# RWKV attention and a SoLU block on one core: w by ScalarE's queue, work moved between engines at the start, and another order at the end

## The chip, the core and the metric

The kernel runs on one core of a Trainium2 chip. A core has five instruction streams: TensorE (PE, the matrix unit; its weight loads are listed apart as PEld), VectorE (DVE), ScalarE (ACT), GpSimd (POOL) and SyncE (SP, which here only issues DMAs). Each stream runs in program order, and streams wait for one another by semaphores. The metric is the time of one execution on the device, in microseconds.

## The reference

The input is r, k, v of shape (4, 8, 768, 48), w and u of shape (8, 48), and the weights of a feed-forward block. Attention first:

```python
state = zeros((B, H, D, D))
for t in range(S):
    cur = einsum('bhd,bhe->bhde', u[None] * k[:, :, t], v[:, :, t])
    y[:, :, t] = einsum('bhd,bhde->bhe', r[:, :, t], state + cur)
    state = w[None, :, :, None] * state + einsum('bhd,bhe->bhde', k[:, :, t], v[:, :, t])
```

Its output, as 3072 rows of 384, then goes through

```python
h = x @ w_in                       # (3072, 1024)
e = exp(h - max(h)); sm = e / (sum(e) + 1e-9)
solu = h * sm
ln = (solu - mean(solu)) / sqrt(var(solu) + 1e-6) * g_ln
out = ln @ w_out                   # (3072, 384)
```

The feed-forward weights arrive as 64-bit floating-point words; the rest is 32-bit.

## The kernel before

The sequence is cut into 24 units (`units`): 6 chunks of 128 time steps for each of 4 batch rows, in the order chunk by chunk. A unit has all 8 heads. Each engine's order is the order of the calls in the code, written out by hand (`tc.manual_schedule()`): there is no planner.

**Preparing.** Powers of w and their inverses are made as tables once (lines 634 to 655): w is loaded into `wq` (line 493), turned by TensorE (`wd_ps`, line 636), and VectorE builds `pw` and `tab` (whose halves are `back` and `fore`) by repeated doubling. TensorE turns `back` into `kdec`, copied by ScalarE (line 665). u is loaded as one row (line 496), spread over 128 rows by a matmul with `ones_row` (line 638) and copied by ScalarE to `u_bc` (line 639). `ident`, the identity matrix, is made by GpSimd, as are the masks. The second halves of six value tiles `vts` are zeroed by ScalarE (line 641). `spin` issues filler matmuls on `ident` whose output nobody reads.

**Attention of a unit.** GpSimd decays k (`decay_k`, line 721) and makes the own products r·u·k (`weigh`, lines 734 and 735); VectorE sums them over each head (`sum_own`, 739). `diagonal` puts the sums on the diagonal of the score matrix: on ScalarE (749) for the first four units, later on GpSimd (754). `turn_r` and `turn_k` turn r and k by TensorE, with a VectorE product (779, 790) or a ScalarE copy (788) on the way out. Scores come from TensorE (801, 819), and VectorE's predicated copies (827, 832) put them above the diagonal. `whole_y` (858) or `merged_y` (881) makes the output, `whole_outer` (922) or `outer` (913) the contribution to the state. In both forms `take_y` copies the transposed result to `xT`.

**Feed-forward of a unit.** `ffn_in` (969) multiplies by w_in; from unit 17 on pairs of units do it with 11 instead of 12 blocks (lines 1003 on). Exponential and sum are ScalarE's (977), solu VectorE's (`unit_a`, 1049 and 1053), the sum of squares ScalarE's (`unit_b`, 1061 or 1065). `deviation` then makes the inverse deviation on GpSimd: a scale and offset (1073), a power of -0.5 (1075), and for units from 4 on a scale and a shift (1079, 1081) which `normalise` (1093) applies on ScalarE. `halve_ln` (1118) splits each 32-bit word in two halves, SyncE issues a turning DMA (1107), and `join_ln` (1112) on VectorE puts the words together. The output product is done for two units at a time with 7 instead of 8 block products (`both_a` to `both_d`, all matmuls on line 1202), which need sums of rows (`row_sums_12`, `row_sums_34`, lines 1192 to 1198).

**Weights.** 14 pieces (6 of w_in, 8 of w_out) are loaded by SyncE (524) and converted to 32 bits in steps: `convert_a` on ScalarE (537), `convert_b` on VectorE (550, 552), `convert_c` on GpSimd (560) and, for w_out alone, `convert_d`, a scaling by -g on ScalarE (568) or VectorE (571). The loop over i = 2 to 6 (line 1390) converts two w_out pieces in each round. Later every piece is loaded again and checked: `check_next` runs ScalarE's sum (582) on one piece and issues the load of the next, `check_least` takes VectorE's minimum (590), and `compare_sums` with `check_sums` ends in one flag, made by a matmul (706).

**Around the change.** At the start the order is: the loads, `ident`, three fillers, tables, u, zeroing, `turn_r(0)`, `turn_k(0)`, `kdec`, `wide` (1313), `weigh(0)`, `decay_k(0)`, and the units 0, 1, 2 interleaved with the conversion of w_in. At the end (lines 1763 to 1821) the last two pairs, 20/21 and 22/23, wait for the norm of unit 23.

Of the kernel before, what the change touches and what calls it, by code (L numbers as in the profile page):

```python
# [399 lines left out]
def direct_path(  # L400
# [89 lines left out]
    w_out_sb = const.tile([128, KF, dm], F32, name="w_out_sb")  # L490
    decays = const.tile([128, HP], F32, name="decays")

    nc.gpsimd.dma_start(out=wq[:, :, 0:D], in_=w.rearrange("(a q) d -> a q d", q=2))
    nc.vector.memset(wq[:, :, D:], 1.0)
    u_row = u_bc[0:1].rearrange("p h d -> p (h d)")
    nc.scalar.dma_start(out=u_row, in_=u.rearrange("h d -> (h d)").unsqueeze(0))
# [66 lines left out]
    def convert_d(j, scalar=False):  # L563
        dst, _, f = pieces[j]
        ma, low = step.pop(j)
        if f is not None:
            if scalar:
                nc.scalar.activation(out=dst, in_=ma.bitcast(F32), func=ACT.Copy,
                                     scale=minus_g[:, f : f + 1])
            else:  # L570
                nc.vector.tensor_scalar_mul(out=dst, in0=ma.bitcast(F32),
                                            scalar1=minus_g[:, f : f + 1])
# [64 lines left out]
    u_ps = psM.tile([128, dm], F32, tag="m", name="u_ps")  # L637
    nc.tensor.matmul(u_ps, ones_row, u_row, start=True, stop=True)
    nc.scalar.copy(out=u_bc.rearrange("p h d -> p (h d)"), in_=u_ps)
    for vt in vts:  # L640
        nc.scalar.activation(out=vt[:, 1].rearrange("p h x -> p (h x)"),
                             in_=ident[:, 0:1].to_broadcast([128, H * P]), func=ACT.Copy, scale=0.0)
    nc.vector.tensor_scalar(out=pw[:, 0, 0], in0=wd_ps, scalar1=LOW, scalar2=HIGH,
# [64 lines left out]

    ones = const.tile([128, 1], F32, name="ones")
    nc.gpsimd.memset(ones, 1.0)  # L710

    live = {}

# [4 lines left out]
    def decay_k(i):  # L718
        X = live.setdefault(i, {})
        X["kp"] = apool.tile([128, H, P], F32, name="kp", bufs=5)  # L720
        nc.gpsimd.tensor_mul(X["kp"].rearrange("p h d -> p (h d)"),  # L721
                             kpads[i % NLD].rearrange("p h d -> p (h d)"),
                             kdec.rearrange("p a d -> p (a d)"))
# [5 lines left out]
                             rpads[i % NLD].rearrange("p h d -> p (h d)"),  # L729
                             rdec.rearrange("p a d -> p (a d)"))  # L730

    def weigh(i, engine):
        rku = live[i]["rku"] = apool.tile([128, H, D], F32, name="rku")
        engine.tensor_mul(rku, kpads[i % NLD][:, :, 0:D], u_bc)  # L734
        engine.tensor_mul(rku, rku, rpads[i % NLD][:, :, 0:D])  # L735

    def sum_own(i):
        own = live[i]["own"] = small.tile([128, H, 1], F32, name="own")
# [329 lines left out]
        unit_a(i)  # L1068
        unit_b(i)

    def deviation(i, j):
        ss, var, rstd = (stats[:, n, i:j] for n in (2, 3, 4))
        nc.gpsimd.tensor_scalar(out=var, in0=ss, scalar1=1.0 / dff, scalar2=1e-6 * dff ** 2,  # L1073
                                op0=ALU.mult, op1=ALU.add)
        nc.gpsimd.tensor_tensor(out=rstd, in0=var, in1=neg_half.to_broadcast([128, j - i]), op=ALU.pow)
        i = max(i, SEVEN)
        if i < j:
            tot, shift, scale, rstd = (stats[:, n, i:j] for n in (1, 2, 3, 4))
            nc.gpsimd.tensor_scalar(out=scale, in0=rstd, scalar1=-float(dff), scalar2=1.0,
                                    op0=ALU.mult, op1=ALU.mult)  # L1080
            nc.gpsimd.tensor_tensor(out=shift, in0=tot, in1=rstd, op=ALU.mult)  # L1081

    def normalise_late(i):
        if SEVEN <= i < N:
# [4 lines left out]
    def normalise(i):  # L1089

        if SEVEN <= i < N:
            solu = live[i]["solu"]
            nc.scalar.activation(out=solu, in_=solu, func=ACT.Identity,  # L1093
                                 scale=stats[:, 3, i : i + 1], bias=stats[:, 2, i : i + 1])
# [26 lines left out]
    def join_ln(i):  # L1121
        X = live[i]
        if i not in ROOM:
            X["lnT"] = fpool.tile([128, KF, 128], F32, name="lnT")
        else:
            X["lnT"] = bigs[ROOM[i]].rearrange("p (f t) -> p f t", f=KF)
        join(X["lnT"], X["turned"])
# [85 lines left out]
    def both_a(i, which=(0, 1, 2)):  # L1213
        X = live[i]
        if 0 in which:
            X["o"], X["o2"] = rows_out(i), rows_out(i + 1)
            X["a"], X["e"] = (psM.tile([128, NH], F32, tag="m", name="o_ps") for _ in range(2))
            block(X["a"], X["lnT"][:, 0:KH], upper[:, :, left], True)
            X.get("copy", nc.scalar.copy)(out=X["o"][:, left], in_=X["a"])
        if 1 in which:  # L1220
            block(X["e"], X["lnT"][:, KH:KF], lower[:, :, left], True)
        if 2 in which:
            block(X["a"], X["s"][2], sums_w[2])
# [8 lines left out]
    def both_b(i, between=None, later=False):  # L1232
        X = live[i]
        block(X["e"], X["s"][1], sums_w[1], True)
        X.get("copy", nc.scalar.copy)(out=X["o2"][:, right], in_=X["e"])
        if not later:
            both_b2(i, between)
# [8 lines left out]
    def both_c_sum(i, also=False):  # L1246
        X = live[i]
        o2 = X["o2"]
        nc.vector.tensor_tensor(out=o2[:, right], in0=X["a"], in1=o2[:, right], op=ALU.add)
        X["summed"] = True  # L1250
        if also:
            o = X["o"]
            nc.vector.tensor_tensor(out=o[:, right], in0=X["e"], in1=o[:, right], op=ALU.add)
            X["summed"] = 2

    def both_c(i):
        X, Y = live.pop(i), live.pop(i + 1)
        ending[i] = X
        o, o2, a, e = (X[n] for n in ("o", "o2", "a", "e"))
        rows, rows2 = (out[ds(b * S + c * T, T)] for b, c in (units[i], units[i + 1]))  # L1260
        if not X.get("summed"):
            nc.vector.tensor_tensor(out=o2[:, right], in0=a, in1=o2[:, right], op=ALU.add)
        block(a, Y["lnT"][:, KH:KF], sums_w[4])
        if i + 2 == N:
            nc.sync.dma_start(out=rows2[:, right], in_=o2[:, right])
        if X.get("summed") != 2:
            nc.vector.tensor_tensor(out=o[:, right], in0=e, in1=o[:, right], op=ALU.add)
        nc.sync.dma_start(out=rows, in_=o)

    def both_d(i):  # L1270
        X = ending.pop(i)
        (b, c), o2, a = units[i + 1], X["o2"], X["a"]
        rows2 = out[ds(b * S + c * T, T)]
        if i + 2 == N:
            nc.vector.tensor_copy(out=o2[:, left], in_=a)
            nc.sync.dma_start(out=rows2[:, left], in_=o2[:, left])
        else:
            nc.scalar.copy(out=o2[:, left], in_=a)
            nc.sync.dma_start(out=rows2, in_=o2)
# [31 lines left out]
    for q in range(2):  # L1311
        rows = slice(q * P, q * P + D)
        nc.gpsimd.tensor_tensor(out=wide.rearrange("p (a q) -> p a q", q=2)[P : P + D, :, q],
                                in0=back[rows, :, 0], in1=pw[rows, 0, 0], op=ALU.mult)
    weigh(0, nc.gpsimd)
    decay_k(0)
    sum_own(0)
    diagonal(0)
# [1 line left out]
    spin(2)  # L1320
    whole_scores(0)
    convert_b(0)
    decay_k(1)
    weigh(1, nc.gpsimd)
    turn_r(1)
    spin(4)
# [63 lines left out]
    for i in range(LA, LA + LO):  # L1390
        j = i - LA
        load(i + 5, "kr")
        load(i + 4, "v")
        if i > LA:
            ffn_in(j)
        before, now = now, [todo.pop(0) for _ in range(2 if todo else 0)]
        turn_r(i + 2)
        turn_k(i + 2)
        for p in before:
            convert_c(p)  # L1400
        for p in now:
            take_up(p)
        if i > LA:
            diagonal(i + 1)
            unit(j)
        for p in before:
            convert_d(p, p % 2)
        sum_own(i + 2)
        decay_k(i + 3)
        if i + 3 >= FIRST:  # L1410
            decay_r(i + 3)
        weigh(i + 3, nc.gpsimd)
        if i - LO >= 0:
            halve_ln(i - LO)
        if i - LO - 1 >= 0:
            join_ln(i - LO - 1)
        if i + 1 < WHOLE:
            whole_scores(i + 1)
            take_scores(i + 1)
        else:  # L1420
            place(i + 1)
            attend([i + 1])
            middle(i + 1)
        if LA < i < WHOLE:
            whole_y(i)
            take_y(i)
            whole_outer(i)
        elif i >= WHOLE:
            merged_y(i)
            take_y(i)  # L1430
        if i > LA:
            update(i)
        else:
            nc.vector.tensor_single_scalar(out=minus_g, in_=g_sb, scalar=-1.0, op=ALU.mult)
        if i + 1 >= WHOLE:
            take_scores(i + 1)
        for p in now:
            convert_b(p)
        halve_rk(i + 3)
# [339 lines left out]
    both_b(l)  # L1779
    unit_a(i)  # L1780
    unit_b(i)
    deviation(i, N)
    halve_ln(j + 1)
    both_c_sum(l)
    both_c(l)
    join_ln(l + 2)
    join_ln(l + 3)
    row_sums_12(l + 2)
    row_sums_34(l + 2, nc.vector)
    both_d(l)  # L1790
    both_a(l + 2, (0,))
    normalise(i)
    halve_ln(i)
    check_next()

# [2 lines left out]
    both_a(l, (1, 2))  # L1798
    take_a(l, "DVE")
    take_a(l, "ACT")  # L1800
    join_ln(l + 2)
    both_b(l)
    check_least()
    both_c(l)
    both_d(l)
    check_next()
    join_ln(l + 3)
    row_sums_12(l + 2)
    check_least()

    l += 2
    both_a(l)
    take_a(l, "DVE")
    take_a(l, "ACT")
    check_least()
    compare_sums()
    row_sums_34(l, nc.vector)
    both_b(l, check_sums)
    both_c(l)
    both_d(l)  # L1820
# [43 lines left out]
```

## Time and profile before

| | us |
|---|---|
| median of three runs | 325.33 (325.25 to 325.44) |
| the profiled execution | 326.05 |
| its span, first to last instruction | 324.3 |
| TensorE busy | 308.9 |
| VectorE busy | 264.6 |
| ScalarE busy | 245.0 |
| GpSimd busy | 250.9 |

A line of an instruction gives its start and length in us, engine, source line, operation, output<-inputs, shape and, in brackets, how long the engine had been idle and what released it. A line of the chain gives start, length, and engine, tile and line; the chain is followed back from the last instruction to whatever released each step. DMA issues are shown with the engine that issues them (a q behind its name). Instructions of one engine may overlap a little in these records[...].

### The profile page before, as it was taken

What the parts mean: (1) busy time and instruction counts of PE and PEld (TensorE: products, weight loads), DVE (VectorE), ACT (ScalarE), POOL (GpSimd) and SP (SyncE); (2) the same over time, 40 slices, a digit from 0 to 9 for tenths busy, and PEclk for the clock granted to TensorE, in tenths of its full rate; (3) what the DMA queues carried; (4) which work ended last, traced back from release to release, by engine and by line L of the source; (5) the groups of instructions that cost most, each with busy time, mean ns of one, the idle gap of its engine ahead of it and who ended that gap; (6) DMA issues with size and microseconds to landing.
All of it is one profiled execution on the core that took longest, in us unless ns stands there. A gap on an engine that the chain in (4) does not pass through costs nothing.

```text
span 324.3 us, 9699 instructions
## 1 busy us (share of the span) xinstructions
PE 308.9 (95%) x3903; PEld 216.7 (67%) x3903; DVE 264.6 (82%) x446; ACT 245.0 (76%) x418; POOL 250.9 (77%) x268
## 2 busy tenths in 40 slices
PE   5999999999999999999999999999999999999972
PEld 3875566555456457677678668668677676779972
DVE  6796999998887979999788699789979945868570
ACT  2875888888559788868968969949969978786410
POOL 4899878889999999999999999979978274275000
PEclk9999999999999999999999999999999999999999
DMA  8999999479999998996999999986757535674821
GB/s 165 255 255 200 207 244 169 75 140 139 194 169 173 174 183 144 159 193 106 167 186 164 176 195 225 197 171 133 143 152 161 92 103 147 144 172 102 166 91 61
DMA packets 165800, 52.64 MB, mean 162 GB/s; under 512 B 158321, under 2 KB 161522, under 8 KB 165746
## 3 DMA queue, kind: packets, MB, share of 16 engines
q1 hardware_dynamic: 165712, 51.92, 82.2%
q8 instruction: 33, 0.54, 0.7%
q14 instruction: 21, 0.17, 0.2%
q0 software_dynamic: 32, 0.00, 0.0%
q10 hardware_dynamic: 2, 0.00, 0.0%
HBM read 26.75 MB, written 4.72 MB: 97 GB/s over the span
## 4 chain that ended last, share of the span: by engine, by line
PE 58%; POOL 17%; DVE 12%; issue 5%; DMA 3%; ACT 2%; SPq 0%; POOLq 0%; ACTq 0%; DVEq 0%
PE o_ps L1202 22%; PE h_ps L969 16%; PE h_part L1003 9%; POOL rp L728 3%; POOL rku L734 3%; POOL big L754 3%; POOL kp L721 3%; PE y_ps L881 2%; PE at L819 2%; POOL rku L735 2%; DVE solu L1053 2%; DVE big L832 2%; DMA raw<-in_moe_w_out_dram 1%; PE y_ps L858 1%; PE h_part L881 1%
## 5 line engine op out<-in xcount | busy, mean ns | idle before, releaser
L969 PE MATMUL h_ps<-w_in_sb,xT 128*128 128x512 f32 x216 | 97.0, 598 | 0.0
L969 PEld LDWEIGHTS h_ps<-w_in_sb,xT 128*128 128x128 f32 x216 | 39.9, 190 | 45.1 <-issue 42.4
L1118 ACT COPY halves<-solu 128x2048 uint16<-128x2048 uint16 x23 | 43.6, 1897 | 1.2 <-DVE stats L1049 1.1
L1112 DVE COPY big<-halves 128x2048 uint16<-128x2048 uint16 x21 | 33.7, 1612 | 2.9 <-DMA halves<-halves 2.7
L721 POOL TENSOR_TENSOR kp<-kpad,kdec 128x512 f32<-128x512 f32 x24 | 34.1, 1423 | 0.7
L1112 DVE COPY lnT<-halves 128x2048 uint16<-128x2048 uint16 x18 | 30.1, 1684 | 1.5 <-DMA halves<-halves 1.4
L735 POOL TENSOR_TENSOR rku<-rku,rpad 128x384 f32<-128x384 f32 x24 | 29.0, 1210 | 1.9
L832 DVE COPY_PREDICATED big<-later_half,at 64x512 f32<-64x512 uint32 x40 | 29.4, 736 | 0.7
L734 POOL TENSOR_TENSOR rku<-kpad,u_bc 128x384 f32<-128x384 f32 x24 | 29.8, 1240 | 0.2
L754 POOL TENSOR_SCALAR_AFFINE_SELECT big<-own 64x512 f32<-64x512 f32 x40 | 27.7, 692 | 1.8
L1202 PE MATMUL o_ps<-w_out_sb,ma 128*128 128x192 f32 x160 | 28.1, 328 | 0.0
L1202 PEld LDWEIGHTS o_ps<-w_out_sb,ma 128*128 128x128 f32 x160 | 26.2, 190 | 1.9 <-issue 1.6
L728 POOL TENSOR_TENSOR rp<-rpad,rdec 128x512 f32<-128x512 f32 x15 | 25.5, 1703 | 0.0
L977 ACT ACTIVATE e<-h_ps 128x1024 f32<-128x1024 f32 x18 | 18.4, 1022 | 8.7 <-PE h_ps L969 8.6
L1073 POOL TENSOR_SCALAR stats<-stats 128x1 f32<-128x1 f32 (+2 forms) x14 | 7.2, 516 | 22.7 <-ACT e L1061 22.0
L1061 ACT ACTIVATE e<-solu,stats 128x1024 f32<-128x1024 f32 x20 | 23.0, 1148 | 2.1 <-DVE solu L1053 2.1
L1053 DVE SCALAR_TENSOR_TENSOR solu<-h_ps,stats,e 128x1024 f32<-128x1024 f32 x18 | 23.1, 1284 | 1.5
L1093 ACT ACTIVATE solu<-solu,stats 128x1024 f32<-128x1024 f32 x17 | 21.0, 1232 | 2.4 <-POOL stats L1081 2.4
L1157 PE MATMUL o_ps<-w_out_sb,lnT 128*128 128x384 f32 x64 | 21.6, 491 | 0.0
L1202 PE MATMUL o_ps<-w_out_sb,lnT 128*128 128x192 f32 x112 | 19.8, 330 | 0.0
L956 POOL TENSOR_TENSOR vt<-vt,wide 48x384 f32<-48x384 f32 x16 | 19.1, 1210 | 0.8
L1202 PEld LDWEIGHTS o_ps<-w_out_sb,lnT 128*128 128x128 f32 x112 | 18.3, 190 | 1.6 <-issue 1.4
(196 smaller groups left out, 703.6 us busy)
## 6 DMA issues: line engine op xcount, KB each, us to landing
raw<-in_moe_w_out_dram SPq DMA_DIRECT2D x16, 384.0 KB, 4.1
kpad<-in_k_dram SPq DMA_DIRECT2D x24, 192.0 KB, 5.0
rpad<-in_r_dram SPq DMA_DIRECT2D x24, 192.0 KB, 5.0
vt<-in_v_dram SPq DMA_DIRECT2D x40, 96.0 KB, 3.7
raw<-in_moe_w_in_dram SPq DMA_DIRECT2D x7, 512.0 KB, 6.3
out_dram<-o SPq DMA_DIRECT2D x18, 192.0 KB, 3.1
raw<-in_moe_w_in_dram SPq DMA_DIRECT2D x10, 256.0 KB, 3.4
out_dram<-kp SPq DMA_DIRECT2D x5, 192.0 KB, 3.0
```

The lines of the kernel that those rows point to most:

```text
L721: nc.gpsimd.tensor_mul(X["kp"].rearrange("p h d -> p (h d)"), kpads[i % NLD].rearrange("p h d -> p (h d)"), kdec.rearrange("p a d -> p (a ...
L728: nc.gpsimd.tensor_mul(X["rp"].rearrange("p h d -> p (h d)"), rpads[i % NLD].rearrange("p h d -> p (h d)"), rdec.rearrange("p a d -> p (a ...
L734: engine.tensor_mul(rku, kpads[i % NLD][:, :, 0:D], u_bc)
L735: engine.tensor_mul(rku, rku, rpads[i % NLD][:, :, 0:D])
L754: nc.gpsimd.affine_select(out=G[rows, c].rearrange("p a q u -> p (a q) u"), in_=X["own"][rows].to_broadcast([U, H, U]), compare_op=ALU.is_ ...
L832: nc.vector.copy_predicated(X["G"][rows, c].rearrange("p a q u -> p q a u"), later_half[rows].unsqueeze(1).to_broadcast([U, 2, HP, U]), X[ ...
L969: nc.tensor.matmul(h_ps[:, ts(n, NX)], X["xT"][:, j, :], w_in_sb[:, j, ts(n, NX)], start=(j == 0), stop=(j == KD - 1))
L1003: nc.tensor.matmul(dst, rows, weights, start=start, stop=True, skip_group_check=True)
L1053: nc.vector.scalar_tensor_tensor(out=solu, in0=X["h"], scalar=rs, in1=X["e"], op0=ALU.mult, op1=ALU.mult, accum_out=tot)
L1112: nc.vector.tensor_copy(out=words.bitcast(U16).rearrange("p n (t o) -> p o n t", o=2), in_=turned)
L1118: copy(out=both.rearrange("p (o n) -> p o n", o=2), in_=split(X["solu"]))
L1202: nc.tensor.matmul(dst, rows[:, f], weights[:, f], start=(start and f == 0), stop=(f == KH - 1), skip_group_check=True)
```

## The change

Seven edits:

1. w is loaded through ScalarE's DMA queue, ahead of u, instead of GpSimd's.
2. ScalarE zeroes four of the six value tiles; GpSimd zeroes the last two, behind its small constants.
3. `weigh` can give its second product to another engine. For unit 0 it is VectorE's.
4. `decay_k(1)` moves ahead of `decay_k(0)`, directly behind `weigh(0)`.
5. All w_out pieces are scaled by ScalarE; four of the eight were VectorE's.
6. `deviation` is cut in three: `variance`, `root` and `shifts`, the first and last on an engine of choice. For unit 23 these are VectorE's, and the power stays on GpSimd.
7. The end is reordered: `join_ln` of unit 20 goes ahead of `variance`, `normalise` of unit 23 ahead of the first part of `both_a` of pair 20, `both_b` ahead of a join, and the last weight check from before the last join to after the second `take_a` of the last pair; `row_sums_34` goes ahead of the minimum and the comparison.

```diff
-    nc.gpsimd.dma_start(out=wq[:, :, 0:D], in_=w.rearrange("(a q) d -> a q d", q=2))
+    nc.scalar.dma_start(out=wq[:, :, 0:D], in_=w.rearrange("(a q) d -> a q d", q=2))
...
-    for vt in vts:
+    for vt in vts[:4]:
         nc.scalar.activation(out=vt[:, 1].rearrange("p h x -> p (h x)"),
...
     nc.gpsimd.memset(ones, 1.0)
+    for vt in vts[4:]:
+        nc.gpsimd.memset(vt[:, 1], 0.0)
...
-    def weigh(i, engine):
-        rku = live[i]["rku"] = apool.tile([128, H, D], F32, name="rku")
+    def weigh(i, engine, second=None):
+        rku = live.setdefault(i, {})["rku"] = apool.tile([128, H, D], F32, name="rku")
         engine.tensor_mul(rku, kpads[i % NLD][:, :, 0:D], u_bc)
-        engine.tensor_mul(rku, rku, rpads[i % NLD][:, :, 0:D])
+        (second or engine).tensor_mul(rku, rku, rpads[i % NLD][:, :, 0:D])
...
+    def variance(i, j, engine):
+        engine.tensor_scalar(out=stats[:, 3, i:j], in0=stats[:, 2, i:j], scalar1=1.0 / dff,
+                             scalar2=1e-6 * dff ** 2, op0=ALU.mult, op1=ALU.add)
+
+    def root(i, j):
+        nc.gpsimd.tensor_tensor(out=stats[:, 4, i:j], in0=stats[:, 3, i:j],
+                                in1=neg_half.to_broadcast([128, j - i]), op=ALU.pow)
+
+    def shifts(i, j, engine):
         i = max(i, SEVEN)
         if i < j:
             tot, shift, scale, rstd = (stats[:, n, i:j] for n in (1, 2, 3, 4))
-            nc.gpsimd.tensor_scalar(out=scale, in0=rstd, scalar1=-float(dff), scalar2=1.0,
-                                    op0=ALU.mult, op1=ALU.mult)
-            nc.gpsimd.tensor_tensor(out=shift, in0=tot, in1=rstd, op=ALU.mult)
+            engine.tensor_scalar(out=scale, in0=rstd, scalar1=-float(dff), scalar2=1.0,
+                                 op0=ALU.mult, op1=ALU.mult)
+            engine.tensor_tensor(out=shift, in0=tot, in1=rstd, op=ALU.mult)
+
+    def deviation(i, j):
+        variance(i, j, nc.gpsimd)
+        root(i, j)
+        shifts(i, j, nc.gpsimd)
...
-    weigh(0, nc.gpsimd)
+    weigh(0, nc.gpsimd, nc.vector)
+    decay_k(1)
     decay_k(0)
...
     convert_b(0)
-    decay_k(1)
     weigh(1, nc.gpsimd)
...
-            convert_d(p, p % 2)
+            convert_d(p, True)
...
     unit_a(i)
     unit_b(i)
-    deviation(i, N)
     halve_ln(j + 1)
     both_c_sum(l)
+    join_ln(l + 2)
+    variance(i, N, nc.vector)
+    root(i, N)
     both_c(l)
-    join_ln(l + 2)
+    shifts(i, N, nc.vector)
     join_ln(l + 3)
     row_sums_12(l + 2)
     row_sums_34(l + 2, nc.vector)
     both_d(l)
+    normalise(i)
     both_a(l + 2, (0,))
-    normalise(i)
     halve_ln(i)
     check_next()
...
     take_a(l, "ACT")
+    both_b(l)
     join_ln(l + 2)
-    both_b(l)
     check_least()
     both_c(l)
     both_d(l)
-    check_next()
     join_ln(l + 3)
     row_sums_12(l + 2)
-    check_least()
...
     take_a(l, "ACT")
+    check_next()
+    row_sums_34(l, nc.vector)
     check_least()
     compare_sums()
-    row_sums_34(l, nc.vector)
     both_b(l, check_sums)
```

More of the change, by code (lines that the diff above doesn't have):

```diff
@@ L1069, in unit @@
         unit_b(i)
[L1071 to L1075, printed above, removed]
+    def variance(i, j, engine):
[5 more added lines that the diff above has]
+    def shifts(i, j, engine):
         i = max(i, SEVEN)
```

## The prediction

> **What bounds the kernel now.** I read the page first (busy shares, chain), then the waits of TensorE, then the order of time in three stretches that the diff touches.
>
> ```profile
> PE 308.9 (95%) x3903; PEld 216.7 (67%) x3903; DVE 264.6 (82%) x446; ACT 245.0 (76%) x418; POOL 250.9 (77%) x268
> ```
>
> TensorE is busy 308.9 of 324.3 us, so only 15.4 us are to be had without removing matmuls. They lie at both ends: the table of stretches gives TensorE 1.65 us in the first 5 us, nothing after 318.8, 3.72 of 5 us in 310 to 315; between 80 and 120 us it is never idle. But some early matmuls are filler (`spin`), so the chain of waits tells more of the start:
>
> ```profile
> 1.45 3.75 DMA wq<-in_w_dram
> 5.60 0.16 DVE pw L643
> 8.03 0.70 DVE tab L654
> 10.49 1.00 POOL rku L735
> 11.52 0.56 DVE own L739
> 12.10 2.17 ACT big L749 x7
> 14.30 1.39 DVE big L827 x2
> 15.73 0.90 PE y_ps L858 x25
> 23.61 5.47 PE h_ps L969 x12
> ```
>
> (Columns: start, length.) The 1.5 KB of w land at 5.20; tables, own products, diagonals and scores follow one another; real work fills TensorE only from 23.6 us. Each microsecond gained ahead of that is worth one, if nothing later holds TensorE back.
>
> In the middle, the waits of TensorE (total, times, longest) show the only repeated stall; the order of time shows the two engines concerned:
>
> ```profile
> PE kv_ps L913 <- DVE big L779: 1.3, 2, 0.7
> 59.91 0.65 DVE L571 TENSOR_SCALAR w_out_sb<-ma,minus_g 128x384 f32<-128x384 f32 x1
> 62.26 0.60 ACT L568 ACTIVATE w_out_sb<-ma,minus_g 128x384 f32<-128x384 f32 x1
> 66.60 1.01 ACT L977 ACTIVATE e<-h_ps 128x1024 f32<-128x1024 f32 x1
> ```
>
> VectorE is busy 4.8 to 4.9 of every 5 us from 35 to 70, but ScalarE has little room too: 4.92 in 60 to 65.
>
> At the end:
>
> ```profile
> 294.97 1.15 ACT L1061 ACTIVATE e<-solu,stats 128x1024 f32<-128x1024 f32 x1 [0.93 <-DVE solu L1053]
> 296.30 2.26 POOL L1073 TENSOR_SCALAR stats<-stats 128x1 f32<-128x1 f32 x1 [3.53 <-ACT e L1061]
> 300.73 1.24 ACT L1093 ACTIVATE solu<-solu,stats 128x1024 f32<-128x1024 f32 x1 [1.44 <-POOL stats L1081]
> 302.01 1.90 ACT L1118 COPY halves<-solu 128x2048 uint16<-128x2048 uint16 x1
> 308.25 1.32 DVE L1112 COPY big<-halves 128x2048 uint16<-128x2048 uint16 x1 [2.12 <-DMA halves<-halves]
> 310.38 0.55 ACT L582 ACTIVATE mag<-raw 128x384 f32<-128x384 f32 x1 [2.98 <-DVE ma L1192]
> 311.28 1.57 PE L1202 MATMUL o_ps<-lows,ma 128*128 128x192 f32 x8 [1.64 <-ACT kp L1219]
> ```
>
> The last row's norm takes 4.4 us on GpSimd (296.30 to 300.71), then a ScalarE pass, a copy, a turning DMA (303.93 to 308.2), a join. TensorE waits 1.64 us. Two waits end together there: ScalarE's L1219 stands behind a weight check whose words landed at 310.3, and VectorE's row sum L1193 ends at 311.03. Removing one alone gives nothing.
>
> **What the skill says.** (1) "DMA: Bandwidth & Descriptors", Specifications: first byte about 1 us on GpSimd's path, 0.6 us on ScalarE's. The trace agrees in direction: w takes 3.75 us from issue to landing; u, issued by ScalarE at 0.80, releases an instruction at 2.13, 1.33 us later. (2) "SBUF — State Buffer", Who interferes with whom: VectorE and GpSimd share one port pair, an exclusive lock. The trace agrees: L552 takes 0.56 us alone and 1.24 to 1.28 when a GpSimd instruction is running, and the 128x1 L1073 above takes 2.26 us beside a VectorE copy against 0.19 at 291.39. (3) "TensorE: Matmul & The Clock Gate", Part 1: the clock doubles after some 3.4 us of activity. Four 128x128 transposes take 1.11 us at 6.98 and 0.66 at 12.44.
>
> **The start.** With w first on ScalarE's queue (0.80) it should land near 2.2, and u, queued behind it, 0.51 us later (its matmul comes after w's transpose anyway). GpSimd loses its 0.81 us issue and the start-up wait, so `ident` begins about 0.8 instead of 2.26; six filler matmuls (0.27 each) end near 3.1, and w's transpose follows. VectorE then is the late one: its own memsets end at 3.67. So the powers start at 3.7 instead of 5.60: 1.9 us. The rest of the table chain, 3.13 us, moves unchanged (5.60 to 8.73 becomes 3.7 to 6.8). GpSimd's `wide` and L734 move with it, L734 ending near 8.5. L735 goes to VectorE: it took 1.00 plus a hop; on VectorE I estimate 0.55, from the two-input L1192 (0.69 for 512 columns): 0.5 us more. Moved `decay_k(1)` stands behind L734 and needs kdec, which ScalarE can copy when TensorE has turned the table, near 8.6. ScalarE itself is free at 7.7: u's copy near 5.1 and four zeroing passes of 0.54 instead of six. The two zeroings on GpSimd are not shown before; between 2 x 0.5 (VectorE's 128x512 memset) and 2 x 0.62 (four 128x128 ones of 0.155), I take 1.1 us, hidden in GpSimd's wait of 3.47 us ahead of `wide`; uncovered they would cost those 1.1. Own products' sum then starts at 9.1 instead of 11.52. **Gain 2.4 us**, carried through diagonal, scores and `whole_y` to the first `ffn_in` if loads allow: the sixth w_in piece, issued at 13.17, needs 8.7 us and lands at 21.9; ScalarE, VectorE and GpSimd convert it in 0.7 + 1.4 + 1.3, at 25.3; TensorE would want it at about 25.4. So nothing is lost, nor is there room for more than 2.6. Lower bound: VectorE's L735 loses the port to `decay_k(1)` (1.28): gain 1.2.
>
> **The middle.** L571 leaves VectorE four times; the next instruction moves up by 0.41, 0.46, 0.57 and 0.38: 1.8 us. ScalarE takes four at 0.51 to 0.62. Up to 57.9, VectorE is 0.87 ahead, so both L913 stalls (0.66 each) should go. But what is late next is ScalarE's exponential L977: in 56.5 to 66.6 ScalarE idles 0.88 (waiting for L1053); the earlier L1053 takes back some 0.7 of it, and the extra scale adds 0.5, so L977 starts at about 66.4, only 0.2 earlier, and TensorE's next h_ps waits for L1053 behind it. TensorE thus keeps about 0.2, plus 0.3 of the L819 stall at 75.1. GpSimd, which the chain shows from 67.2 to 121.7, starts on L560 released by VectorE's L552, about 1 us sooner, so that stalls of 0.31 and 0.52 at 128.9 and 140.2 shrink. **Gain 0.9**, bounds -1.0 (each late exponential on the path) and +2.1 (the whole 1.3 + 0.3 + 0.5).
>
> **The end.** `variance` on VectorE (0.15) stands behind the moved join L1112 (295.15 to 296.45) and so follows L1061 at once; the power alone stays on GpSimd (0.56 at 291.66, 1.08 beside a copy), with VectorE idle behind it; `shifts` is two ops of 0.15. Ready at 297.6 instead of 300.7. Queued behind `shifts` are join 21 and the row sums: about 0.25 us later, and TensorE with them. ScalarE finishes halves(22) and L1278 at 298.2, so L1093 starts there, 2.5 earlier; L1219 of the next pair is now between it and L1118, which starts at 299.8 instead of 302.0. SyncE's queue has two output stores ahead of the turn (done at 301.5); the turn is issued at 301.7, lands at 306.0 (4.3 us, as measured). Join and two sums end at 309.1. The weight check L582 no longer stands ahead of L1219: it comes after `take_a`, and its words, issued behind the turn near 303.6, land 4.5 later. TensorE reaches the block at 309.75 and finds both: 311.28 becomes 309.75, 1.5 us. The check's chain (0.75 + 0.55 + 0.82) now ends near 313.6, where TensorE's L706 comes at 313.7; I subtract 0.1. **Gain 1.4**, bounds 0.4 and 1.7. The tail after 318.4 is unchanged. Handing the early deviations through three functions changes no instruction.
>
> **Sum.** 2.4 + 0.9 + 1.4 = 4.7. The profiled execution took 326.05 (span 324.3 and 1.75 around it): 321.35. The median 325.33 is 0.72 below that execution: **320.6**.
>
> **Rivals.** *Port and landing:* the start keeps 1.2; total 3.5, 321.8. For it: L552's doubled rows; kdec is ready only 0.1 after L734 ends. Against: kpad1 lands at 2.80 + 5.8 = 8.6, so GpSimd can't take the port earlier. *ScalarE becomes the bound:* the middle gives -1.0, total 2.8, 322.5. For it: 4.92 of 5 busy; against: 0.7 to 1.1 us idle ahead of L977 in the first iterations. *The DMA holds the start:* its queues are full from 5 to 20 us; if w_in lands no earlier and conversions queue up behind it, the start keeps 0.1; total 2.4, 322.9. *Slower:* filler is unchanged but real work comes sooner; if TensorE's clock dropped back in a gap, some 8 us of its rows between 10.7 and 23.6 would double: 325.3 - 4.7 + 8 = 328.6; it decides from about 5 us on. Against: my gaps there are under 0.5 us. *Everything works and ScalarE has room:* 2.5 + 2.1 + 1.7, 319.0.
>
> **Chances.** Forecast (319.4 to 321.7) 0.58; port 0.13; ScalarE 0.13; DMA 0.06; the best case 0.06; slower 0.04. The range 319.0 to 322.9 takes in all but the slower one and the worst of the others. 0.2% (0.65 us) is about what a measurement tells from no change: faster 0.93, same 0.03, slower 0.04.
>
> **Signs.** Right: L643 near 3.7, L739 near 9.1, the first y_ps near 13.2, h_ps near 21.2; no wait of L913; L977 waiting less; L1093 near 298 less the shift; no wait at the last L1202. Wrong: L735 over 0.9 us, ScalarE without idle and h_ps waiting for L1053, raw words waited for, L706 waited for.

## The result

| | before | after |
|---|---|---|
| median (range) of 6 executions each, us | 325.46 (325.25 to 326.1) | 322.82 (321.68 to 324.0) |
| the profiled execution, us | 326.05 | 321.73 |
| its span, us | 324.3 | 320.0 |

The ratio is 0.9906, 95% interval 0.9887 to 0.9926, a gain of 3.1 us (2.4 to 3.7). Between the medians it is 2.6 us and between the profiled executions 4.3 us; the forecast was 4.7. The executions of the changed kernel spread over 2.3 us, those of before over 0.85.

The edits put a few new lines in, so line numbers moved: 735 is now 737, 739 is 741, 779 is 781, 788 is 790, 801 is 803, 858 is 860, 881 is 883, 892 is 894, 913 is 915, 969 is 971, 977 is 979, 1049 and 1053 are 1051 and 1055, 1061 is 1063, 1073 is 1074, 1075 is 1078, 1093 is 1104, 1112 is 1123, 1118 is 1129, 1193 is 1204, 1202 is 1213, 1219 is 1230.

First the page, the busy time of each engine:

```profile
PE 307.5 (96%) x3903; PEld 216.8 (68%) x3903; DVE 262.9 (82%) x446; ACT 245.9 (77%) x420; POOL 245.6 (77%) x265
```

The same number of matmuls stands in 4.3 us less. Of these, 2.9 us are idle time of TensorE and 1.4 us are busy time (308.9 to 307.5); 0.6 of the 1.4 lie ahead of the first feed-forward matmul, where some matmuls ran faster. The order of time at the start (start, length, engine, line, operation, output<-inputs, shape, idle before and releaser):

```profile
0.79 1.27 ACTq L493 DMA_DIRECT2D wq<-in_w_dram  x1
2.10 0.27 ACTq L496 DMA_DIRECT2D u_bc<-in_u_dram  x1
4.10 0.24 PE L636 MATMUL wd_ps<-ident,wq 4*128 4x4 f32 x1 [1.04 <-DMA wq<-in_w_dram]
4.37 0.16 DVE L643 TENSOR_SCALAR pw<-wd_ps 128x4 f32<-128x4 f32 x1 [0.71 <-PE wd_ps L636]
4.53 1.61 PE L638 MATMUL u_ps<-u_bc,ones_row 1*128 1x384 f32 x2 [0.20 <-DMA u_bc<-in_u_dram]
9.21 0.56 DVE L737 TENSOR_TENSOR rku<-rku,rpad 128x384 f32<-128x384 f32 x1 [0.32 <-POOL rku L736]
9.81 0.55 DVE L741 TENSOR_REDUCE own<-rku 128x8 f32<-128x384 f32 x1
13.84 1.15 PE L860 MATMUL y_ps<-big,vt 128*32 128x128 f32 x30
21.02 0.30 PE L860 MATMUL y_ps<-big,vt 128*32 128x128 f32 x2 [1.04 <-issue]
```

w's issue alone takes 1.27 us and u queues behind it. The powers start at 4.37 instead of 5.60, so 1.23 of the forecast's 1.9 us. VectorE's product L737 takes 0.56 us, where 0.55 was estimated. The first `y_ps` comes 1.43 earlier (13.84 for 15.27). Then TensorE stands still for 1.04 us in the middle of the second unit's y matmuls, released by nothing that the profile shows ("issue"); before, the same place cost 0.18:

```profile
15.27 1.42 PE L858 MATMUL y_ps<-big,vt 128*32 128x128 f32 x30
21.84 0.30 PE L858 MATMUL y_ps<-big,vt 128*32 128x128 f32 x2 [0.18 <-issue]
```

The first feed-forward matmul comes at 22.73 for 23.54: 0.81 us are left.

The middle, first from the waits of TensorE (total, times, longest), then from the order of time:

```profile
PE y_ps L883 <- ACT big L790: 0.7, 1, 0.7
PE kv_ps L915 <- DVE big L781: 0.3, 1, 0.3
PE kv_ps L915 <- ACT xT L894: 0.2, 1, 0.2
```

```profile
60.68 1.10 ACT L568 ACTIVATE w_out_sb<-ma,minus_g 128x384 f32<-128x384 f32 x2
65.53 1.02 ACT L979 ACTIVATE e<-h_ps 128x1024 f32<-128x1024 f32 x1
66.66 0.57 ACT L790 COPY big<-tk_ps 128x512 f32<-128x512 f32 x1
67.28 1.10 PE L883 MATMUL y_ps<-big,vt 112*32 112x64 f32 x64 [0.69 <-ACT big L790]
```

The first of the two waits for VectorE (0.66 us each) shrank to 0.28. The second is gone; in its place TensorE waits 0.16 us for ScalarE's copy to `xT` and then 0.69 us for a ScalarE copy that stands behind the exponential.

The end:

```profile
294.06 0.55 POOL L1078 TENSOR_TENSOR stats<-stats,neg_half 128x1 f32<-128x1 f32 x1 [3.73 <-DVE stats L1074]
294.71 0.15 DVE L1087 TENSOR_TENSOR stats<-stats 128x1 f32<-128x1 f32 x1
295.68 1.24 ACT L1104 ACTIVATE solu<-solu,stats 128x1024 f32<-128x1024 f32 x1
297.02 1.90 ACT L1129 COPY halves<-solu 128x2048 uint16<-128x2048 uint16 x1
297.70 1.54 PE L1213 MATMUL o_ps<-lows,ma 128*128 128x192 f32 x8 [0.56 <-DVE ma L1204]
303.62 1.33 DVE L1123 COPY big<-halves 128x2048 uint16<-128x2048 uint16 x1
307.03 1.46 PE L1213 MATMUL o_ps<-lows,ma 128*128 128x192 f32 x8
311.03 0.19 PE L706 MATMUL n_ps<-ones,low 128*1 128x1 f32 x2
```

ScalarE's L1063 ahead of this norm starts 2.44 us earlier than L1061 did before (292.53, 294.97); add 2.44 to compare with before. The norm of the last row takes 1.0 us, from VectorE's scale and offset at 293.84 to 294.86, instead of 4.4; the join ends at 304.95 instead of 309.57 and TensorE's block, 311.28 before, starts at 307.03 with no wait ahead of it. Nor does L706 wait.

TensorE's lead over before adds up: 0.81 us at the first feed-forward matmul, 1.84 at 143.6 us of before (1.03 more), 2.5 at 218 (0.7 more, nearly all because an "issue" wait of 0.77 us of before at 214.7 is missing here), 4.25 at the last block (1.75 more).

### The profile page after: what moved, and what is told of

Read it like the earlier page. It is cut to its first block, busy times and chain, and to the rows that moved or that the text cites. A ratio compares the mean times of both kernels' runs of the same rounds, so it can differ in the third digit from the quotient of the medians.

```text
span 320.0 us, 9698 instructions
## 1 busy us (share of the span) xinstructions
PE 307.5 (96%) x3903; PEld 216.8 (68%) x3903; DVE 262.9 (82%) x446; ACT 245.9 (77%) x420; POOL 245.6 (77%) x265
## 4 chain that ended last, share of the span: by engine, by line
PE 79%; DVE 10%; ACT 4%; issue 2%; POOL 1%; DMA 1%; ACTq 0%; DVEq 0%; POOLq 0%
PE o_ps L1213 25%; PE h_ps L971 25%; PE h_part L1005 8%; PE o_ps L1168 7%; PE y_ps L883 3%; PE at L821 3%; DVE big L1123 2%; DVE solu L1055 2%; PE kv_ps L915 1%; PE h_part L883 1%; DVE big L834 1%; PE y_ps L860 1%; PE tr_ps L780 1%; ACT big L751 1%; ACT e L979 1%
## 5 line engine op out<-in xcount | busy, mean ns | idle before, releaser
L737 POOL TENSOR_TENSOR rku<-rku,rpad 128x384 f32<-128x384 f32 x23 | 28.9, 1257 | 1.8
L736 POOL TENSOR_TENSOR rku<-kpad,u_bc 128x384 f32<-128x384 f32 x24 | 28.8, 1202 | 0.2
L1063 ACT ACTIVATE e<-solu,stats 128x1024 f32<-128x1024 f32 x20 | 23.0, 1148 | 2.9 <-DVE solu L1055 2.8
L1078 POOL TENSOR_TENSOR stats<-stats,neg_half 128x1 f32<-128x1 f32 (+2 forms) x14 | 14.6, 1045 | 4.8 <-DVE stats L1074 3.7
```

The source lines that it names most:

```text
L737: (second or engine).tensor_mul(rku, rku, rpads[i % NLD][:, :, 0:D])
```

## The experiments

The parts have the numbers of the seven edits above. All gains are against the kernel before on the same chip, by the ratio.

### Which part brings what

The theory was that the start lost its gain and the other two parts kept theirs.

Parts 1 to 4 alone:

> Edits 1 to 4 alone (w by ScalarE's queue, two zeroings on GpSimd, second own product of unit 0 on VectorE, decay_k(1) first). Theory A (the term of the start was mis-sized: 1.7 us gained up to the second y_ps, half of it lost when TensorE waits for its next instructions): 0.5 to 1.0 us faster than before, with executions further apart than those of before, and a wait of about 1 us of TensorE near 20 us that ends with nothing the profile shows. Rival B (the start keeps its 1.7, and what is missing in the median is lost in the middle, by ScalarE): 1.7 us faster, executions close together.

Part 5 alone, the one line with `convert_d`:

> Edit 5 alone (all w_out pieces scaled by ScalarE). Theory A: about 0.9 us faster, as forecast; the first L913 stall of 0.66 goes, the second is replaced by a wait behind ScalarE. Rival B: no gain or up to 1.0 us slower, and executions as far apart as those of the whole change.

Parts 6 and 7 alone:

> Edits 6 and 7 alone (norm of unit 23 on VectorE, reordered end). Theory A: 1.8 us faster (the two profiles differ by that from 288 us on), executions as close together as before. Rival B: 1.4 us or less, since the profiled execution of the whole change was its best one.

The whole change, beside these three:

> The changed kernel once more, for a second profile and more times. Theory A: 321.7 to 324.0 us again; an execution of about 323 us has a longer wait of TensorE for instructions in the first 25 us, and the same end. Rival B: the longer executions differ in the stretch from 55 to 75 us.

| | ratio to before (95%) | gain, us | forecast, us |
|---|---|---|---|
| start, 1 to 4 | 0.9986 (0.997 to 1.0002) | 0.5 (-0.1 to 1.0) | 2.4 |
| scalings, 5 | 0.9977 (0.9968 to 0.9986) | 0.75 (0.5 to 1.0) | 0.9 |
| end, 6 and 7 | 0.9944 (0.9928 to 0.996) | 1.8 (1.3 to 2.35) | 1.4 |
| all | 0.9911 (0.9894 to 0.9928) | 2.9 (2.35 to 3.5) | 4.7 |

(Gains: one less the ratio, times 325.95, the median of before on that chip.) The parts add up, 3.0 to 2.9; within these intervals they don't take anything from one another. Nearly all that is missing is missing at the start. This execution of the whole change shows more of it: the span is 321.4 us where the other had 320.0, and by the order of time w and above all u land later,

```profile
4.46 0.24 PE L636 MATMUL wd_ps<-ident,wq 4*128 4x4 f32 x1 [1.40 <-DMA wq<-in_w_dram]
5.24 1.61 PE L638 MATMUL u_ps<-u_bc,ones_row 1*128 1x384 f32 x2 [0.55 <-DMA u_bc<-in_u_dram]
6.78 0.47 PE L780 MATMUL tr_ps<-ident,rpad 128*128 128x128 f32 x1
22.06 0.30 PE L860 MATMUL y_ps<-big,vt 128*32 128x128 f32 x2 [0.93 <-issue]
```

so that `tr_ps` starts 0.7 us later than in the first execution, the first `y_ps` 1.2 later (15.07), and when the first feed-forward matmul starts (23.77) nothing is left of the start's gain. From `tr_ps` to the first `y_ps` TensorE has no idle time in either execution, so a later start of this row of matmuls delays `y_ps` directly. The other 0.5 us of the 1.2 is the pace of the matmuls, which comes up again below.

In the middle, the waits of TensorE with part 5 alone show that the trade belongs to this part:

```profile
PE y_ps L881 <- ACT big L788: 0.7, 1, 0.7
PE kv_ps L913 <- DVE big L779: 0.3, 1, 0.3
```

### The start: landing, or something behind it?

w alone on ScalarE's queue (part 1):

> Edit 1 alone: w first on ScalarE's queue, u behind it; everything else as before. What the traces suggest so far: w lands about 1.1 us sooner, u about 2.3 us later, so that the first power starts 0.9 to 1.2 us earlier than at 5.60, but TensorE's instruction wait near 21 us (0.18 before) takes 0.5 or more of it. Then 0.0 to 0.5 us faster than before. Rival: edit 1 is worth its 1.9 us of the forecast and edits 2 to 4 lose it again; then 1.0 to 1.9 us faster, more than all four start edits together (0.45 us).

0.9981 (0.9954 to 1.0008), 0.6 us (-0.3 to 1.5). The first power starts at 4.36. Parts 2 to 4 on top of part 1 show no gain: 0.5 us for all four against 0.6 for this one, each within the other's interval. The traces show where it went. From the first power to the own sum it is 5.92 us with part 1 alone (4.36 to 10.28) and 5.43 us with all four (4.66 to 10.09), so the 0.5 us that the forecast gave to part 3 is there. But w landed 0.3 us later in the second of these executions, and the wait marked "issue" took 0.93 us instead of 0.45, so that the first feed-forward matmul does not gain (22.58 against 22.87).

The changed kernel with w's transfer replaced by a constant (it leaves out w, so its output is another):

```diff
-    nc.scalar.dma_start(out=wq[:, :, 0:D], in_=w.rearrange("(a q) d -> a q d", q=2))
+    nc.vector.memset(wq[:, :, 0:D], 0.9)
```

> The changed kernel without the transfer of w: VectorE writes the constant 0.9 into its tile instead, so the output isn't the reference's; u is then alone on ScalarE's queue. It shows what the start would give if w were there at once, as the forecast put it. Both theories: the first power at 3.7 us instead of 4.37, u's matmul near 4 us, the scores and the second whole_y 0.7 to 1.2 us earlier than in the changed kernel. Theory A (TensorE's next instructions are the late thing): the wait marked issue in the 449th TensorE instruction grows from 1.0 to 1.6 us or more, the first h_ps comes at most 0.4 us earlier, and the time is at most 0.4 us below the changed kernel's, a ratio of 0.990 to 0.992. Theory B (only w's and u's landing was mis-sized): the wait stays near 1.0, h_ps comes 0.7 to 1.2 us earlier, a ratio near 0.988.

0.9872 (0.9824 to 0.992): 4.2 us (2.6 to 5.7), 1.3 more than the whole change had beside the parts, though the intervals overlap. First power at 3.62, first `y_ps` at 13.18, the wait 0.84, first `h_ps` at 21.95, 0.78 earlier than in the changed kernel's first trace. This fits theory B better: the late landing is on the path. But A is not gone: the wait marked "issue" is still there.

To get the early landing without leaving w out, w can be brought in fewer runs. As one row, spread by GpSimd and turned by four one-row matmuls (`w_row` is a view of one row of `kdec`, `wq` one of `rdec`):

```diff
-    nc.scalar.dma_start(out=wq[:, :, 0:D], in_=w.rearrange("(a q) d -> a q d", q=2))
+    nc.scalar.dma_start(out=w_row, in_=w.rearrange("h d -> (h d)").unsqueeze(0))
...
+    nc.gpsimd.tensor_copy(out=wq[:, :, :, 0:D],
+                          in_=w_row.rearrange("o (a q d) -> o a q d", a=HP, q=2))
...
-    nc.tensor.transpose(wd_ps, wq.rearrange("a q d -> a (q d)"), ident[0:HP, 0:HP])
+    for a in range(HP):
+        nc.tensor.matmul(wd_ps[:, a : a + 1], rdec[0:1, a], ones_row[:, 0:1], start=True, stop=True)
```

> The changed kernel with w brought as one row of 1.5 KB into one partition (an issue like u's, 0.3 to 0.5 us instead of 1.27 us), spread by a GpSimd copy of 384 elements to the padded row and turned by four one-row matmuls instead of one transpose; the output stays the reference's. If the price was the issue of w in eight runs, with u behind it, w lands near 2.2 us, the copy ends near 2.8, the first power starts at 3.7 to 3.9 instead of 4.37, u's matmul near 3.6; then 0.6 to 1.3 us faster than the changed kernel run beside it, a ratio to before of 0.987 to 0.989. Rival: u and w land late because the loads of k and r run beside them, however they are issued; then the first power stays at 4.2 or later and the time within 0.3 us of the changed kernel.

Beside it the changed kernel again:

> The changed kernel once more, beside the two above, for a comparison on one chip: 322 to 323 us, a ratio of 0.990 to 0.992 to before.

0.9892 (0.9864 to 0.992) against 0.9891 (0.9853 to 0.993) for the changed kernel: nothing gained. The order of time shows that the landing worked and my price for the matmuls was wrong:

```profile
0.79 0.53 ACTq L496 DMA_DIRECT2D kdec<-in_w_dram  x1
1.35 0.21 ACTq L499 DMA_DIRECT2D u_bc<-in_u_dram  x1
2.38 0.49 POOL L617 COPY rdec<-kdec 1x384 f32<-1x384 f32 x1 [0.87 <-DMA kdec<-in_w_dram]
3.00 1.86 PE L642 MATMUL wd_ps<-ones_row,rdec 1*128 1x1 f32 x8
```

The issue fell from 1.27 to 0.53 us, the row was there by 2.4, but the eight one-column passes (two for each of the four matmuls) took 1.86 us where the single transpose takes 0.24. The first power started at 4.90.

So: four runs of 384 B, a GpSimd copy, and the transpose kept:

```diff
-    nc.scalar.dma_start(out=wq[:, :, 0:D], in_=w.rearrange("(a q) d -> a q d", q=2))
+    nc.scalar.dma_start(out=w_rows, in_=w.rearrange("(a q) d -> a (q d)", q=2))
...
+    nc.gpsimd.tensor_copy(out=wq[:, :, 0:D], in_=w_rows.rearrange("a (q d) -> a q d", q=2))
```

> The changed kernel with w brought in four runs of 384 B into four partitions and spread to the padded tile by a GpSimd copy (about 0.2 us), then turned by the one transpose as before; the output stays the reference's. If the price is in the eight runs of w's issue (1.27 us), the issue takes 0.6 to 0.9 us, the copy ends near 2.9 to 3.2, the first power starts at 3.6 to 3.9 and u's matmul near 3.5 to 4.2; then 0.5 to 1.2 us faster than the changed kernel, a ratio to before of 0.986 to 0.989. Rival: w's landing with the copy behind it gives nothing over 4.37; then within 0.4 us of the changed kernel, 0.989 to 0.992.

```profile
0.79 0.57 ACTq L495 DMA_DIRECT2D kdec<-in_w_dram  x1
2.35 0.25 POOL L616 COPY wq<-kdec 4x96 f32<-4x96 f32 x1 [0.86 <-DMA kdec<-in_w_dram]
3.52 0.15 DVE L646 TENSOR_SCALAR pw<-wd_ps 128x4 f32<-128x4 f32 x1
20.75 0.30 PE L862 MATMUL y_ps<-big,vt 128*32 128x128 f32 x2 [1.47 <-issue]
22.46 1.55 PE L973 MATMUL h_ps<-w_in_sb,xT 128*128 128x512 f32 x3
```

0.9848 (0.9814 to 0.9882), a median of 321.31 us (321.3 to 322.31): 5.0 us (3.85 to 6.1) faster than before, with w loaded. Its median is below all three of the changed kernel (322.82, 323.0, 321.94) and its interval below two of its three, though the two kernels were not run side by side here. Its fastest execution (321.3) is no faster than the changed kernel's (321.4); what differs is that five of its six lie within 0.2 us of that. The powers start at 3.52 and the first `y_ps` at 12.64, 2.63 us earlier than before: the forecast's 2.4 is reached there. And then TensorE waits 1.47 us, and `h_ps` keeps 1.08.

Part of these 2.63 us is not the landing. The 32 score matmuls of the first unit took, in the changed kernel's first and second trace, without the transfer of w, and with four runs:

```profile
9.68 1.64 PE L803 MATMUL at<-big 48*64 48x128 f32 x32
10.39 1.97 PE L803 MATMUL at<-big 48*64 48x128 f32 x32
8.84 1.82 PE L803 MATMUL at<-big 48*64 48x128 f32 x32
8.68 1.09 PE L805 MATMUL at<-big 48*64 48x128 f32 x32
```

It is the change of pace that the prediction read from four transposes, 1.11 us at first and 0.66 later; one matmul takes some two thirds of its time from about 10.8, 12.6, 10.4 and 8.5 us on in these four traces (a filler 0.275 us for 0.421), so ahead of the scores in the last of them, and in or behind them in the others. TensorE had then worked without a gap for 3.2 us in the last and for 5.1 to 7.4 in the others, where the prediction had some 3.4. Without the transfer of w and with four runs `tr_ps` starts alike (5.26 and 5.27), and yet the first `y_ps` is 0.54 us apart. With parts 1 to 4 alone, which have the changed kernel's start, the scores took 1.16 us. So the pace differs between executions of the same start, and what sets its moment was not tried.

### What the wait marked "issue" is

The last question is what that wait is. It comes in the middle of one group of matmuls whose operands are there. The filler groups, n matmuls of 128 columns each, were made one matmul of n times 128 columns, on top of the one-row kernel:

```diff
-        for _ in range(n):
-            nc.tensor.matmul(ps[:, 0:128], ident, ident, start=True, stop=True)
+        nc.tensor.matmul(ps[:, 0 : 128 * n].rearrange("p (n x) -> p n x", n=n), ident,
+                         ident.unsqueeze(1).to_broadcast([128, n, 128]), start=True, stop=True)
```

> As w_row, and each filler group of n 128-column matmuls becomes one matmul of n x 128 columns: the same columns, about 40 TensorE instructions fewer ahead of the wait near 20 us. If that wait is TensorE's instruction stream running out, it belongs to the 449th instruction counted from the start, not to a piece of work: it will stand some 40 instructions later in the work, among the state's matmuls or the next scores, still released some 2.4 us after the first 16 KB instruction packet, and the time is within 0.4 us of w_row. Rival: it is a hidden wait of the y matmuls; then it stays at the same two matmuls of y_ps.

0.9905 (0.9879 to 0.9931), no different from the one-row kernel. The one-row kernel's own trace has no wait of 0.15 us or more there: its 220th matmul record starts at 20.40, 2.4 us behind its packet (18.00). With fewer fillers the wait is back, short, and at a later place in the work than in the other traces, among the state's matmuls:

```profile
20.82 0.28 PE L864 MATMUL y_ps<-big,vt 128*32 128x128 f32 x2
20.85 0.33 PE L928 MATMUL kv_ps<-vt,kp 128*32 128x48 f32 x5
21.34 0.45 PE L928 MATMUL kv_ps<-vt,kp 128*32 128x48 f32 x21
```

(0.15 us idle ahead of 21.34.) Counted from the start, it stands in front of the 220th matmul record, as in the kernel before, where that is a y matmul (in two traces, no transfer of w and four runs, it is the 221st). In all twelve traces where the wait shows (0.15 us or more), it ends 2.3 to 2.6 us after the first 16,384-byte packet on the queue that the page lists as q8, kind "instruction":

| | first `y_ps` | first packet of q8 | wait ends | wait |
|---|---|---|---|---|
| before | 15.27 | 19.34 | 21.84 | 0.18 |
| after, first trace | 13.84 | 18.63 | 21.02 | 1.04 |
| after, second | 15.07 | 19.57 | 22.06 | 0.93 |
| after, third | 14.24 | 18.36 | 20.80 | 0.47 |
| no transfer of w | 13.18 | 17.77 | 20.25 | 0.84 |
| four runs of w | 12.64 | 18.27 | 20.75 | 1.47 |

The Trainium skill's "Runtime: NRT & Kernel Launch", Instruction fetch mechanics, says that instructions come in 16 KiB blocks of 256, fetched ahead over the engine's own DMA queue, at a cost "mostly hidden". The block is seen here; hidden it is not. TensorE's work ahead of the wait came earlier, the packet by far less: between before and the last row the work is 2.63 us earlier, the packet 1.07. The wait is what opens between the two; where the packet came earlier too, as without the transfer of w (17.77), it did not grow (0.84). The second wait of this kind, near 214 us, behaves alike: in nine of the traces TensorE waits 0.18 to 0.85 us in front of the 2884th record, and the wait ends 2.4 to 2.7 us after a 16,384-byte packet of the same queue. So the packet is what both waits go with; that a late block causes them is inferred from this, since no run moved the packet by itself. Why the packet starts when it does was not tried. The DMA engines are nine tenths busy or more with loads from 5 to 20 us in both kernels, and that they hold it back is only argued.

### The end: two waits or one?

Parts 6 and 7 with the weight check left where it was, and then the check alone moved:

```diff
     both_d(l)
+    check_next()
     join_ln(l + 3)
     row_sums_12(l + 2)
+    check_least()
```

(This is against the changed end; `check_next` goes from its new place.)

> Edits 6 and 7 without moving the weight check: the last row's norm shared with VectorE, join and matmuls reordered, but the check still ahead of ScalarE's L1219. Theory (two waits end together, removing one gives nothing): TensorE still waits some 1.5 us for kp L1219 near 309 to 311; only the 0.39 us stall of before at the row is gone: 0.2 to 0.6 us faster than before. Rival: the norm's row was the only wait, the check isn't: 1.4 to 1.9 us faster, as all end edits together (1.8 us).

The other one is against the kernel before, and takes `row_sums_34` along:

```diff
     both_d(l)
-    check_next()
     join_ln(l + 3)
     row_sums_12(l + 2)
-    check_least()
...
     take_a(l, "ACT")
+    check_next()
+    row_sums_34(l, nc.vector)
     check_least()
     compare_sums()
-    row_sums_34(l, nc.vector)
```

> Only the weight check is moved behind the last turn's row sums; the norm stays on GpSimd. Theory (removing one of the two alone gives nothing): TensorE then waits for VectorE's row sum L1193 instead, from 309.6 to 311.0: 0.0 to 0.3 us faster than before. Rival: the check alone was the wait: 1.0 us or more.

The norm without the check's move: 0.9953 (0.9937 to 0.997), 1.5 us (1.0 to 2.05) of the 1.8. The check's move alone: 0.9999 (0.9978 to 1.002), nothing; TensorE then waits for the row sum, as expected:

```profile
311.10 1.54 PE L1202 MATMUL o_ps<-lows,ma 128*128 128x192 f32 x8 [1.52 <-DVE ma L1193]
```

For the norm the rival was right. SyncE's queue and ScalarE in that kernel:

```profile
301.20 2.42 SPq L1116 DMA_TRANSPOSE halves<-halves  x1
303.71 0.57 SPq L524 DMA_DIRECT2D raw<-in_moe_w_out_dram  x1
```

```profile
307.27 0.56 ACT L582 ACTIVATE mag<-raw 128x384 f32<-128x384 f32 x1 [0.29 <-DMA raw<-in_moe_w_out_dram]
307.96 0.32 ACT L1228 COPY kp<-o_ps 128x192 f32<-128x192 f32 x1
```

The load of the check's words stands behind the last turn on SyncE's queue. Before, the two were issued at:

```profile
303.93 1.78 SPq L1107 DMA_TRANSPOSE halves<-halves  x1
305.81 1.07 SPq L524 DMA_DIRECT2D raw<-in_moe_w_out_dram  x1
```

A turn that is issued earlier brings the words earlier, so ScalarE's copy is done at 308.3, ahead of TensorE's block at 309.06. The two waits had one cause, the late norm.

## Why the prediction was right or wrong

**The sum.** 325.33 less 4.7 gave 320.6; it measured 322.8, inside the range of 319.0 to 322.9, 0.1 us from its upper end, and outside the 319.4 to 321.7 that was given to the forecast itself. Middle and end held within 0.5 us; that the end brought 0.4 more than forecast hides some of the loss. The start failed: 0.5 us for 2.4.

**The step that failed: "With w first on ScalarE's queue (0.80) it should land near 2.2, and u, queued behind it, 0.51 us later (its matmul comes after w's transpose anyway)."** The landing was taken from u, one run of 1.5 KB issued in 0.51 us. w goes out in eight runs of 192 B to four partitions; its issue takes 1.27 us, its packets move from 2.78 to 2.97, and TensorE is released at 4.10. u's issue can't start before 2.10. Its matmul does come after w's transpose, but TensorE waits for it there: `u_ps` starts at 4.53 to 5.24 instead of 4.3 to 4.7, where TensorE was free, and the 1.6 us that it takes stand ahead of `tr_ps`. With the issue cut to 0.57 us (four runs) the powers started at 3.52, where the forecast had 3.7, and the own sum at 9.06, where it had 9.1. The first `y_ps` then came at 12.64 and not at 13.2; these 0.5 us are the pace, which the forecast did not count on. The bulk loads' own first packets start at 1.90 us in these traces. The four runs of w moved from 1.74 to 2.00, ahead of most of them, the eight runs in the middle of them; how much of the late landing is the issue and how much the loads was not separated. The Trainium skill's "DMA: Bandwidth & Descriptors", Queues, rings and completion order, adds that a transfer's semaphore write lands only behind every earlier write of the same DMA engine. The traces agree in direction: from w's last flag packet to TensorE's release it is 1.13 us at 2.97, with the loads running, and from the last one of the four runs, at 2.00, to GpSimd's 0.35.

**What the sum left out.** TensorE's instructions. The trace of before had 0.18 us of "issue" at 21.84 and I didn't ask what it was; the DMA was looked at for w_in only. Over those 0.18 this wait took 0.86 us in the first trace and 1.29 with four runs of w. The rival "the DMA holds the start" named 0.1 us as what is left, nearer to the measured 0.5 (-0.1 to 1.0) than the forecast's 2.4, but by w_in, and the conversions of w_in were not what TensorE waited for.

**Parts 2 to 4.** L737 at 0.56 us was right to 0.01, so the port rival did not come true. But its case did not occur either: `decay_k(1)` waited for `kdec` and started at 9.60, behind L737 at 9.21, and in the other traces with part 3 this product started first too. What VectorE would have lost to a GpSimd instruction that was there before it is not shown. The slower rival falls; no part was measurably slower than before. The zeroings on GpSimd (0.98 us for two, 1.1 forecast) were hidden.

**The middle.** 0.9 forecast, 0.75 (0.5 to 1.0) measured. That ScalarE's exponential would be late next was right, but by another way than given: L977 started at 66.80 with part 5 alone, not at 66.4, and it was the kT copy behind it, not VectorE's L1053, that TensorE waited for. The sign "no wait of L913" did not come: 0.28 us for VectorE stayed, and 0.16 for ScalarE came. The stall at 128.9 went, the one at 140.2 stayed at 0.52.

**The end.** 1.4 forecast, 1.8 (1.3 to 2.35). The norm's chain held: with the shift of 2.44 taken out, L1093 was forecast at 298.2 and came at 298.12, the last join at 306.0 and came at 306.06. TensorE was not delayed by the 0.25 us given to the row sums: a wait of 0.56 for L1204 took the place of the 0.39 for the join, and its lead hardly changed (2.51 us at 218, 2.49 behind that wait). The 0.1 for L706 did not come either. "Removing one alone gives nothing" was right for the check and wrong for the norm, which brings 1.5 alone; SyncE's queue had been read for the turn and not for what the turn holds back.

**The execution.** The 4.7 was made against one profiled execution, and the gain between the profiled executions is 4.3. Of that, some 0.7 us is the second wait marked "issue": 0.77 us before, 0.60 in the second trace of the changed kernel, none in the first.

## What to carry to other kernels

Before pricing a small transfer by another one of the same size, count its runs and read its issue: 1.5 KB cost 1.27 us in eight runs and 0.53 in one, and what is queued behind it pays too. A wait marked "issue" in the middle of a matmul group deserves a question, since what is gained ahead of it can be lost in it: 0.18 us before, up to 1.47 here. When two waits end together, follow each back along its queue: the same late transfer may stand ahead of both.

## What was not expected of the hardware

- The wait that goes with TensorE's instruction block cost up to 1.47 us at its 220th matmul record and ended 2.3 to 2.6 us after the packet, which moved by 1.07 us where the work moved by 2.63.
- Issue of w on ScalarE's queue: 1.27 us in eight runs of 192 B, 0.57 in four of 384 B, 0.53 in one; of u behind it, one run, 0.21 to 0.27, and 0.51 as the first.
- Eight one-column passes with one-row weights took 1.86 us, about 0.23 each, as long as the whole 4x128 transpose (0.24).
- The same w and u landed up to 0.7 us apart between executions of one kernel (`u_ps` at 4.53, 4.91 and 5.24).
- The same 32 score matmuls took 1.09 to 1.97 us from one trace to another, 1.16, 1.64 and 1.97 with the same start of the kernel.
